# A spectral filter dealt between the matmuls of a gated MLP: its column step dealt first with pauses, down products in runs of 3, 3 and 2, and evictions and copies issued in another order

## The chip, the cores and the metric

The kernel runs on one core of a Trainium2 chip. The time is the device time of one execution in microseconds. Before the change it was 1312.53 us (median of 3 runs, 1312.05 to 1313.11). TensorE (PE) multiplies matrices, VectorE (DVE) and ScalarE (ACT) do elementwise work, GpSimd (POOL) and SyncE (SP) here only issue transfers (POOL also a few fills).

## The reference

```python
x = A_x                                   # 1 x 2048 x 576
g = _sigmoid((x * gate_w).sum(-1, keepdims=True))
a = irfft2(rfft2(x) * (w_r + 1j * w_i))   # over 2048 x 576
b = einsum(gelu(x @ w_gate) * (x @ w_up), w_down)   # hidden width 4608
return g * a + (1 - g) * b
```

Two results are mixed by a gate for each token: `a` filters the tokens in the two-dimensional Fourier domain, `b` is a gated MLP with a tanh GELU.

## The kernel before, in words

**The matmuls.** Each fp32 operand is split into a high and a low part (12 bits each), and a product is made of three matmuls, high by high, low by high and high by low. The MLP goes over two halves of the tokens (`p`), and for each over 18 blocks of 256 hidden features (`i`). The first two blocks of the first half are done plainly (`normal`, L1597). The other 34 are done in `products` (L1408): the gate and up projections of a block by seven products of sums and differences of quarters (`a11 a12 s2 s3 s1 a22 s4`, a scheme of Strassen's kind, n = 0 to 6) in place of eight. One product is two halves (s = 0, 1), each of seven matmuls with 512 columns (`seven`, L1392). Products n = 0, 2 and 3 are copied out of PSUM by ScalarE (L1478): n = 0 into another PSUM tile, from which later products go on, n = 2 and 3 into SBUF (`u`, `u3`, tiles `xraw`). Product 1 accumulates into the PSUM tile of product 0 after that was copied, and product 3 into that of product 2. `finish` (L1422) queues gelu, multiplication and the split of the hidden tile.

**Downs.** The hidden tiles of a block wait in `pend` and are multiplied by `w_down` during the next block: eight downs (`down`, L995), each for 128 tokens and of 12 matmuls with 288 columns into a PSUM tile `pdn`, of which there are two. ScalarE evicts it, scaled by 1 - g, into one of four staging tiles `stg` (L1011), and a transfer issued on POOL adds that to the result in DRAM (`put`, L982). The tuple `downs` (L1448) says how many downs follow each product: 1,1,1,1,1,1,2 in most blocks, 0,0,0,0,0,1,1 in the first of the 34 (`opening`) and 2,2,2,2,2,0,0 in the last (`end`).

**The order of work.** The order of every engine's instructions is written out by this program. After each half product and each down, `gap` (L782) is called; it counts gaps and deals out other work (`dealt`, L788): first all that `at(n, fn)` (L774) put off to this gap, then work from a generator, paid from a credit. `tick` adds 1.08 times the estimated TensorE time to the credit, VectorE work takes its estimated cost off, and the credit is capped (2.0, in the column stage 2.4). A generator yields a cost, or None when it wants to go on only at a later gap. The generator (`branch`, L1585) does the whole spectral part: row transforms on VectorE, columns, inverse rows, and last the adds of `a` to the result (`adds`, L703). What is left of it is dealt without limit in the last block, at n = 5 (L1493).

**The column stage** (`columns`, L290). The transform over tokens is finished in 16 steps `kb`. A step makes a first complex product on TensorE (`product`, L347: six matmuls with 290 columns, also into a `pdn` tile), copies it out, combines it on VectorE (L431 to L433), turns it by 90 degrees on ScalarE (`turned`, L248), multiplies by the filter (L443, L444), adds (L450 to L452), and splits the result for a second product, which is made in the next step (L438) and copied out at L441. L446 to L457 prepare the operand of the next step. Beside it a second generator (`beside`, L381, in `side`) does the radix-4 column butterflies (`column_four`, L253) and twiddles (`column_twiddles`, L269) of the tiles to come and of those done; a step waits at L447 until its tiles are made. While this stage runs (`ops["ahead"]`), `dealt` takes from the side work first, and from the step only if credit is left (L798 to L817). Evictions of downs are then not issued in `down` but kept in `post`, which is emptied at the end of the gap or just before the turn (L435). Otherwise `down` issues the eviction itself, ahead of its gap.

Of the kernel before, what the change touches and what calls it, by code (L numbers as in the profile page):

```python
# [27 lines left out]
ROWS = 5120  # L28
UNIT = ROWS // 4
RATE = 1.08  # L30
STEP = 8
FIRST = 2
APART = (13, 14, 16, 17)
PAIRS = ((2, 3, 4, 5), (6, 7, 8, 9), (10, 11, 12, 13), (14, 15, 16, 17), (0, 1))
# [126 lines left out]
def _build(nc, tc, a):  # L161
    with ExitStack() as ctx:
# [72 lines left out]
        def copy(o, i):  # L235
            act.activation(o, i, AF.Copy)  # L236
# [53 lines left out]
        def columns():  # L290
# [52 lines left out]
            def step(us=0.0):  # L343
                credit[0] -= us
                yield None
# [75 lines left out]
            for kb in range(16):  # L421
                was, more = kb > 0, kb + 1 < 16
                v = product(0, kb, xh, xl)
                if was:
                    copy(yh, vs)
                yield from step()
                copy(zr, v[:, 1, :NK])
                copy(t0, v[:, 0, :NK])
                yield from step()
                if was:  # L430
                    vec.tensor_tensor(yl, vs, f(yh), ALU.subtract)  # L431
                vec.tensor_tensor(zi, t0, zr, ALU.subtract)
                vec.tensor_tensor(zr, t0, zr, ALU.add)  # L433
                yield from step(1.67 if was else 0.91)
                while post:  # L435
                    post.pop(0)()
                turned(vs, z, 1.0)
                u = product(1, kb - 1, yh, yl) if was else None  # L438
                yield from step()
                if was:  # L440
                    copy(two(tile_of(kb - 1)), u[:, :, :NK])  # L441
                    done[0] = kb - 1
                vec.tensor_tensor(z, z, w0, ALU.mult)  # L443
                vec.tensor_tensor(vs, vs, w1, ALU.mult)  # L444
                yield from step(1.52)
                if more:  # L446
                    while made[0] < (kb + 1) // 4:  # L447
                        yield None
                    copy(xh, tile_of(kb + 1))
                vec.tensor_tensor(z, z, vs, ALU.add)  # L450
                vec.tensor_tensor(vs2[:, 0], zr, zi, ALU.add)
                vec.tensor_tensor(vs2[:, 1], zr, zi, ALU.subtract)  # L452
                at(1, lambda kb=kb: load_ww(kb + 1, 0))
                at(2, lambda kb=kb: load_ww(kb + 1, 1))
                yield from step(1.67)
                if more:
                    vec.tensor_tensor(xl, tile_of(kb + 1), f(xh), ALU.subtract)  # L457
                yield from step(0.76)
                yield from waits(STEP - 7)
            copy(yh, vs)  # L460
            yield None
            vec.tensor_tensor(yl, vs, f(yh), ALU.subtract)
# [325 lines left out]
        def dealt():  # L788

            count[0] += 1  # L790
            while later and later[0][0] <= count[0]:
                later.pop(0)[1]()
            if aux:
                aux.pop(0)()
            credit[0] = min(credit[0], cap[0])
            if not gens:
                return
            ahead = side and ops.get("ahead")  # L798
            while ahead and credit[0] > 0:
                v = next(side[0], None)  # L800
                if v is None:
                    break
                credit[0] -= v
            while credit[0] > 0:
                try:
                    v = next(gens[0])
                except StopIteration:
                    gens.pop(0)
                    v = None
                if v is None:  # L810
                    while side and not ahead and credit[0] > 0:
                        v = next(side[0], None)
                        if v is None:
                            break
                        credit[0] -= v
                    return
                credit[0] -= v  # L817
# [177 lines left out]
        def down(prev, t):  # L995

            p, i, tb = prev[:3]
            u = 8 * p + 4 * tb + t
            v = ps_dn()
            for part in range(2):  # L1000
                down_mm((v[:, 0, 0:HD], v[:, 1, 0:HD]), prev, t, part)
            if t == 3:
                for _, hold, _ in prev[3]:
                    h = hold[0]
                    if any(h is x for x in base + extra):
                        free_h.append(h)
            if p == 0 and i == 0 and tb == 0:
                copy(held(u).rearrange("p (c k) -> p c k", c=2), v[:, :, 0:HD])
            else:
                assert ops.get('released', 0) > min(dnn[0], 3)  # L1010
                out = lambda: put(u, lambda o: act.activation(o.rearrange("p (c k) -> p c k", c=2), v[:, :, 0:HD], AF.Copy,  # L1011
                                                              scale=omg[:, u:u + 1]), i == 0, i)
                if ops.get("ahead"):
                    post.append(out)
                else:
                    out()
            behind[0] = t % 2 == 0
            gap()
            behind[0] = False
# [388 lines left out]
        def products(b, k):  # L1408
# [4 lines left out]
            made = {}  # L1413
            opening, end, turn = k == 0, k == len(b.groups) - 1, (p, i) == (0, NBLK - 1)
            if opening:
                at(6, lambda: credit.__setitem__(0, credit[0] - 2.0))
                for q in range(2 * len(PAIRS) - 2):
                    t = (free_low[:, 0:7 * P] if q % 2 == 0 else wtb[:, 0:7 * P]).rearrange("p (m k) -> p m k", m=7)
                    for n, fn in zip((-4, 6, 8, 9, 10), tail_piece(q + 2, t)):
                        at(max(1, n + 12 * q), fn)  # L1420
# [25 lines left out]

            fore, acc = ([f() for f in fs] for fs in ((ps_gu, ps_gu), (lambda: ps_x(0), lambda: ps_x(1)))[::1 - 2 * (k % 2)])
            downs = (0, 0, 0, 0, 0, 1, 1) if opening else (2, 2, 2, 2, 2, 0, 0) if end else (1, 1, 1, 1, 1, 1, 2)  # L1448
            for n, (name, nd) in enumerate(zip(("a11", "a12", "s2", "s3", "s1", "a22", "s4"), downs)):
                m = n + 3  # L1450
                b.prep(k + m // 7, m % 7)
# [20 lines left out]
                    fore = [ps_x(s) for s in range(2)] if k % 2 else [ps_gu() for _ in range(2)]  # L1472
                ps = acc if n in (2, 3, 5) else fore
                for s in range(2):
                    soon = opening and n in (0, 2)
                    b.seven(ps[s], k, n, name, s, n in (0, 4), (lambda n=n, s=s: copy((acc, None, u)[n][s], ps[s])) if soon else None)
                    if n in (0, 2, 3) and not soon:
                        copy((acc, None, u, u3)[n][s], ps[s])  # L1478
                    elif n in (4, 6):
                        at(0 if end else 1, lambda x=(u3, u)[n // 2 - 2][s], y=ps[s]: add(x, y))  # L1480
# [6 lines left out]
                    at(2, lambda name=name: swap(name))  # L1487
                if n in (1, 4, 5, 6):
                    finish(*{1: ("c11", fore, gl[0]), 4: ("c22", u3, u3[0]), 5: ("c21", acc, gl[1]), 6: ("c12", u, u[0])}[n])
                for _ in range(nd):  # L1490
                    if pend:
                        down(*pend.pop(0))
# [214 lines left out]
```

## Time and profile before

The profiled execution took 1312.65 us, its span (first to last instruction) 1310.9 us. Busy time by stretch, in us:

| stretch | what runs beside the MLP | PE | DVE | ACT | granted PE clock | share of DMA time |
|---|---|---|---|---|---|---|
| 100 to 558 | row transforms, operands of the second half | 458.00 | 418.03 | 287.79 | 1.00 | 0.90 |
| 558 to 912 | column stage and what follows it | 349.60 | 285.21 | 264.36 | 1.00 | 0.98 |
| 912 to 1250 | inverse rows | 338.00 | 315.50 | 195.72 | 1.00 | 0.86 |
| 1250 to 1311 | last adds, last block, end | 56.47 | 29.93 | 23.08 | 0.98 | 0.90 |

How to read the lines that follow. A line of a view of groups has the source line, the engine, the operation, what it writes and reads, shapes and count, then busy time and the mean of one in ns, then the idle time before it with what ended that. A line of the waits has who waited for whom, the total in us, how often, and the longest. A line of a timeline has the start, the time until the end of the last of the merged instructions, the instruction and the count, and idle time in brackets. A line of the chain of waits has start and length. The ends of matmuls are modelled, so the pace of TensorE is read from starts. L236 is the helper `copy` on ScalarE, so copies are told apart by their tiles.

### The profile page before, as it was taken

How to read it: one execution, taken by the hardware profiler on the slowest of the kernel's cores; microseconds unless marked ns; L12 is line 12 of the kernel's file. 1: busy time of each engine (PE TensorE's matmuls, PEld its weight loads, DVE VectorE, ACT ScalarE, POOL GpSimd, SP SyncE). 2: the span in 40 equal slices, each digit the busy share in tenths (PEclk: the TensorE clock that was granted, in tenths of full speed). 3: DMA queues.
4: the chain of work that ended last, by engine and by line, in shares of the span. 5: the costliest groups of instructions: out<-in, count | busy, mean ns of one | idle time of the engine just before them, and what ended most of it. 6: DMA issues, size and time to landing. Idle time of an engine off the chain costs nothing.

```text
span 1310.9 us, 20543 instructions
## 1 busy us (share of the span) xinstructions
PE 1299.9 (99%) x7210; PEld 1150.1 (88%) x7210; DVE 1134.5 (87%) x1734; ACT 831.6 (63%) x1405; POOL 307.7 (23%) x392
## 2 busy tenths in 40 slices
PE   9999999999999999999999999999999999999998
PEld 7888888888888888888888888888888888888888
DVE  7899999988999998778888878778999977999954
ACT  5665655657565667678687878766555566565552
POOL 0011212122221211124321333333331231212151
PEclk9999999999999999999999999999999999999999
DMA  9779999897777799969988999999997798877797
GB/s 350 240 204 235 263 257 244 190 286 138 138 145 146 143 320 367 296 174 272 398 250 202 217 258 222 252 224 209 176 184 152 140 217 206 182 158 141 150 188 194
DMA packets 202537, 285.94 MB, mean 218 GB/s; under 512 B 18177, under 2 KB 118657, under 8 KB 201665
## 3 DMA queue, kind: packets, MB, share of 16 engines
q0 software_dynamic: 64848, 110.13, 49.4%
q1 hardware_dynamic: 137152, 174.06, 40.9%
q8 instruction: 56, 0.92, 0.3%
q10 hardware_dynamic: 432, 0.44, 0.1%
q14 instruction: 49, 0.39, 0.1%
HBM read 157.87 MB, written 137.88 MB: 226 GB/s over the span
## 4 chain that ended last, share of the span: by engine, by line
PE 86%; DMA 5%; DVE 4%; ACT 3%; issue 1%; SPq 1%; DVEq 0%; ACTq 0%
PE pdn L978 31%; PE px L1399 22%; PE pgu L1399 22%; PE px L1401 4%; PE pgu L1401 4%; DMA gub<-tails 1%; PE pdn L351 1%; DMA ye<-stg 1%; DMA gub<-ws 1%; DMA home<-rows 1%; ACT gub L236 0%; DMA tmp<-rows 0%; ACT stg L1011 0%; DMA low<-wgu 0%; DVE gub L1383 0%
## 5 line engine op out<-in xcount | busy, mean ns | idle before, releaser
L1011 ACT ACTIVATE stg<-pdn,omg 128x576 f32<-128x576 f32 x276 | 204.6, 741 | 328.8 <-PE pdn L978 182.5
L993 POOL DMA_DIRECT2D yd<-stg x232 | 202.1, 871 | 778.4 <-ACT stg L1011 752.6
L978 PE MATMUL pdn<-dn,hb 128*128 128x288 f32 x1356 | 199.9, 294 | 1.6 <-ACT rows L236 1.4
L978 PEld LDWEIGHTS pdn<-dn,hb 128*128 128x128 f32 x1356 | 191.7, 188 | 10.7 <-ACT rows L236 2.1
L1399 PE MATMUL pgu<-xhi,gub 128*128 128x512 f32 x480 | 149.0, 392 | 0.0
L1399 PE MATMUL pgu<-til,gub 128*128 128x512 f32 x516 | 132.1, 391 | 1.0 <-ACT xraw L236 1.0
L978 PEld LDWEIGHTS pdn<-dn,ext 128*128 128x128 f32 x816 | 122.2, 188 | 9.3
L978 PE MATMUL pdn<-dn,ext 128*128 128x288 f32 x816 | 129.3, 294 | 0.0
L978 PE MATMUL pdn<-dn,gub 128*128 128x288 f32 x816 | 129.3, 294 | 0.0
L1383 DVE TENSOR_TENSOR gub<-low,gub 128x512 fp32r<-128x512 f32 x151 | 103.4, 685 | 17.5 <-ACT gub L236 15.6
L978 PEld LDWEIGHTS pdn<-dn,gub 128*128 128x128 f32 x816 | 115.4, 188 | 0.0
L1399 PEld LDWEIGHTS pgu<-til,gub 128*128 128x128 f32 x516 | 94.4, 188 | 19.1 <-ACT xraw L236 1.2
L236 ACT ACTIVATE gub<-low 128x512 fp32r<-128x512 f32 (+1 forms) x163 | 100.7, 619 | 12.3 <-DMA low<-wgu 6.1
L1399 PE MATMUL px<-xhi,gub 128*128 128x512 f32 x344 | 106.9, 392 | 1.2 <-DVE gl L1427 0.7
L1399 PE MATMUL px<-til,gub 128*128 128x512 f32 x396 | 101.2, 391 | 0.0
L1399 PEld LDWEIGHTS pgu<-xhi,gub 128*128 128x128 f32 x480 | 86.6, 188 | 14.6
L1399 PE MATMUL pgu<-xlo,gub 128*128 128x512 f32 x240 | 93.6, 390 | 0.0
L1399 PEld LDWEIGHTS px<-til,gub 128*128 128x128 f32 x396 | 72.5, 188 | 13.7
L1399 PEld LDWEIGHTS px<-xhi,gub 128*128 128x128 f32 x344 | 62.0, 188 | 12.3 <-DVE gl L1427 1.2
L978 PE MATMUL pdn<-dn,hx 128*128 128x288 f32 x444 | 70.3, 294 | 0.0
L1401 PE MATMUL pgu<-til,gub 128*128 128x512 f32 x172 | 67.1, 390 | 0.4 <-DMA gub<-tails 0.4
L1399 PE MATMUL px<-xlo,gub 128*128 128x512 f32 x172 | 67.1, 390 | 0.0
(311 smaller groups left out, 2758.6 us busy)
## 6 DMA issues: line engine op xcount, KB each, us to landing
yd<-stg POOLq DMA_DIRECT2D x232, 288.0 KB, 5.4
low<-ws SPq DMA_DIRECT2D x114, 256.0 KB, 5.4
gub<-tails SPq DMA_DIRECT2D x179, 128.0 KB, 4.9
gub<-wd SPq DMA_DIRECT2D x68, 288.0 KB, 5.4
tails<-wtb SPq DMA_DIRECT2D x28, 448.0 KB, 5.6
ye<-stg POOLq DMA_DIRECT2D x32, 288.0 KB, 5.5
yd<-ye POOLq DMA_DIRECT2D x32, 288.0 KB, 7.4
slot<-tails SPq DMA_DIRECT2D x59, 128.0 KB, 4.6
```

The costliest lines, as they stand in the source:

```text
L236: act.activation(o, i, AF.Copy)
L351: pe.matmul(v[:, al, :NK], cc[d][2 * al + q], two(x)[:, al], start=n == 0, stop=n == 2)
L978: pe.matmul(ps[half], h[:, l, c], d[:, q, half * HD:(half + 1) * HD], start=part == 0 and n == 0, stop=part == 1 and n == 2)
L993: pl.dma_start(yd[u], o, accum_op=ALU.add)
L1011: out = lambda: put(u, lambda o: act.activation(o.rearrange("p (c k) -> p c k", c=2), v[:, :, 0:HD], AF.Copy, scale=omg[:, u:u + 1]), i == ...
L1383: vec.tensor_tensor(v[:, 0:5:4], x, f(v[:, 1:4:2]), ALU.subtract)
L1399: pe.matmul(ps, l, x[:, t], start=first and t == 0 and q == 0, stop=False, skip_group_check=True)
L1401: pe.matmul(ps, w[:, 512 + P * s:512 + P * (s + 1)], xt, start=False, stop=True, skip_group_check=True)
```

## The change

In the column stage the step gets three pauses: `yield None` ahead of the emptying of `post` and the turn, `yield None` between the copy out of the second product and the multiplications, and, as before, one at the step's end. `dealt` takes one piece of the step first, in every gap and whatever the credit, and then side work for the credit that is left. Outside that stage the eviction of a down is put off by `at(1, out)`: it is still issued in the gap behind its down, but behind what was already put off to that gap. In all blocks the copies of products 0, 2 and 3 are issued inside `seven`, ahead of their gap (before, only those of 0 and 2 in the opening block were; the others came behind the gap). The downs come behind products 1, 4 and 6, in runs of 3, 3 and 2, except in the opening and the last block and while the column stage runs. In the opening block 1.5 us more are taken off the credit at gap 10.

```diff
-STEP = 8
...
                 yield from step(1.67 if was else 0.91)
+                yield None
                 while post:
                     post.pop(0)()
                 turned(vs, z, 1.0)
...
                 if was:
                     copy(two(tile_of(kb - 1)), u[:, :, :NK])
                     done[0] = kb - 1
+                yield None
                 vec.tensor_tensor(z, z, w0, ALU.mult)
                 vec.tensor_tensor(vs, vs, w1, ALU.mult)
...
                 yield from step(0.76)
-                yield from waits(STEP - 7)
+                yield None
...
             if not gens:
                 return
-            ahead = side and ops.get("ahead")
-            while ahead and credit[0] > 0:
-                v = next(side[0], None)
-                if v is None:
-                    break
-                credit[0] -= v
+            if side and ops.get("ahead"):
+                credit[0] -= next(gens[0]) or 0.0
+                while side and credit[0] > 0:
+                    v = next(side[0], None)
+                    if v is None:
+                        break
+                    credit[0] -= v
+                return
             while credit[0] > 0:
...
                 if v is None:
-                    while side and not ahead and credit[0] > 0:
+                    while side and credit[0] > 0:
...
                 if ops.get("ahead"):
                     post.append(out)
                 else:
-                    out()
+                    at(1, out)
...
             if opening:
-                at(6, lambda: credit.__setitem__(0, credit[0] - 2.0))
+                for n, us in ((6, 2.0), (10, 1.5)):
+                    at(n, lambda us=us: credit.__setitem__(0, credit[0] - us))
...
             downs = (0, 0, 0, 0, 0, 1, 1) if opening else (2, 2, 2, 2, 2, 0, 0) if end else (1, 1, 1, 1, 1, 1, 2)
+            popped = 0
...
-                    soon = opening and n in (0, 2)
-                    b.seven(ps[s], k, n, name, s, n in (0, 4), (lambda n=n, s=s: copy((acc, None, u)[n][s], ps[s])) if soon else None)
+                    soon = n in (0, 2, 3)
+                    b.seven(ps[s], k, n, name, s, n in (0, 4), (lambda n=n, s=s: copy((acc, None, u, u3)[n][s], ps[s])) if soon else None)
...
+                if not (opening or end):
+                    nd = (n + 1 + n // 6 if ops.get("ahead") else (0, 3, 3, 3, 6, 6, 8)[n]) - popped
+                    popped += max(0, nd)
                 for _ in range(nd):
                     if pend:
                         down(*pend.pop(0))
```

## The prediction

> **What bounds the kernel now.** I read the page's head first, then the waits of TensorE, then the chain of waits.
>
> ```profile
> span 1310.9 us, 20543 instructions
> PE 1299.9 (99%) x7210; PEld 1150.1 (88%) x7210; DVE 1134.5 (87%) x1734; ACT 831.6 (63%) x1405; POOL 307.7 (23%) x392
> ```
>
> TensorE is busy 99% of the span, so nothing on another engine counts unless it makes TensorE wait. The next view lists such waits behind the start.
>
> ```profile
> PE pdn L978 <- ACT rows L236: 1.4, 3, 0.5
> PE pgu L1399 <- ACT xraw L236: 1.0, 1, 1.0
> PE px L1399 <- DVE gl L1427: 0.7, 1, 0.7
> PE px L1399 <- DVE slot L1383: 0.5, 1, 0.5
> PE px L1399 <- ACT pgu L236: 0.5, 1, 0.5
> PE pgu L1401 <- DMA gub<-tails: 0.4, 1, 0.4
> PE pdn L351 <- DVE tmp L457: 0.2, 1, 0.2
> ```
>
> L1383 is in the opening block. The other six lines (eight waits, 4.2 us shown) all lie in or just behind the column stage. The chain of waits, whose long pieces are pairs of downs, says what that stage loses in all.
>
> ```profile
> 133.41 3.16 PE pdn L978 x24
> ...
> 168.43 3.16 PE pdn L978 x24
> ...
> 553.57 3.16 PE pdn L978 x24
> ...
> 937.21 3.16 PE pdn L978 x24
> ```
>
> ```profile
> 586.12 0.97 PE L351 MATMUL pdn<-tmp,xtl 128*128 128x290 f32 x6
> 586.93 0.56 PE L978 MATMUL pdn<-dn,ext 128*128 128x288 f32 x3
> ```
>
> A block without disturbance takes 35.02 us (133.41 to 168.43). From 553.57 to 937.21 there are ten blocks in 383.64 us: ten times 35.02 is 350.2, and 32 column products at 0.81 (586.12 to 586.93) are 25.9. So 7.5 us are lost there. That, and what an undisturbed block can save, is all this change can win.
>
> **Runs of downs.** Nothing is removed: 8 downs and 98 product matmuls a block stay. What changes is how often TensorE goes from one kind to the other. First a pair and a single down with the product behind each, then products with no down between.
>
> ```profile
> 133.25 3.32 PE L978 MATMUL pdn<-dn,hb 128*128 128x288 f32 x24
> 136.41 0.63 PE L1399 MATMUL pgu<-xhi,gub 128*128 128x512 f32 x2
> ...
> 139.63 1.74 PE L978 MATMUL pdn<-dn,hb 128*128 128x288 f32 x12
> 141.20 0.63 PE L1399 MATMUL pgu<-xhi,slot 128*128 128x512 f32 x2
> ...
> 144.40 0.30 PE L978 MATMUL pdn<-dn,hb 128*128 128x288 f32 x1
> ```
>
> ```profile
> 87.13 1.52 PE L1399 MATMUL px<-til,slot 128*128 128x512 f32 x6
> ...
> 91.89 0.62 PE L1399 MATMUL px<-xhi,gub 128*128 128x512 f32 x2
> ```
>
> By the starts, three half products without a down take 4.76, or 3.17 for a whole one. Behind a single down it is 3.20 (141.20 to 144.40), behind a pair 3.22 (136.41 to 139.63), and the pair takes 3.16 where two singles take 3.14. So a single run costs 0.03 and a pair 0.07. A block loses 6 x 0.03 + 0.07 = 0.25 now. A run of three is not in the trace: if its product pays as behind a pair, it costs 0.05 and some 0.03 for its two joints; if the cost grows on, 0.08 + 0.04; if joining is free, 0.05. Two of these and a pair make 0.23, 0.31 or 0.17. Over 24 blocks (34, less opening, end and eight in the column stage) that is a gain of 1.9 to a loss of 1.4. I take 0.23, nearest to the row of the pair: a gain of 0.02 x 24 = 0.5 us.
>
> [...]
>
> **What hides the closed gaps.** With three downs in a row, the third needs the first one's PSUM tile (two exist), so ScalarE's eviction must be done within one down. The trace of before has no third down, but a pair followed by a product gives the time it would have.
>
> ```profile
> 239.87 0.96 PE L978 MATMUL pdn<-dn,hb 128*128 128x288 f32 x6
> ...
> 241.46 0.63 PE L1399 MATMUL px<-xhi,slot 128*128 128x512 f32 x2
> ```
>
> ```profile
> 240.12 0.74 ACT L1011 ACTIVATE stg<-pdn,omg 128x576 f32<-128x576 f32 x1 [3.03 <-issue]
> ```
>
> ```profile
> L1011 ACT ACTIVATE stg<-pdn,omg 128x576 f32<-128x576 f32 x105 | 78.0, 743 | 144.9 <-PE pdn L978 82.3 <-issue 56.4 <-ACT gub L236 2.6
> ```
>
> The first down ends at 239.87, its eviction runs from 240.12 to 240.86, and a third down would start at 241.46: 0.60 to spare, 0.54 after the 0.06 that a release takes (below). The group is that of 100 to 558 us: 144.9 us idle before 105 evictions, nearly all of it for TensorE, so ScalarE usually stands ready. Copying "a gap on" puts this gap's own ScalarE work (a gelu, a high part) ahead of the eviction; it can run while the down is still on, so it costs nothing unless ScalarE is behind. Then what is queued behind the eviction is late too, and TensorE waits.
>
> The products now also follow each other with no down between: the second accumulates into the PSUM tile that ScalarE copies after the first, one half product (1.59) later. A heavy place shows it, TensorE (the half behind the copied one) first, then ScalarE.
>
> ```profile
> 252.63 1.52 PE L1399 MATMUL pgu<-til,gub 128*128 128x512 f32 x6
> ```
>
> ```profile
> 252.38 1.41 ACT L236 ACTIVATE tmp<-rows 128x289 f32<-128x289 f32 x2
> 253.68 0.60 ACT L236 ACTIVATE xraw<-pgu 128x512 f32<-128x512 f32 x1
> ```
>
> The copy ends at 254.28, and with no down the half that needs it would start 1.59 after 252.63, at 254.22: late. Issued ahead of those two row copies it could start at 252.88 (0.25 behind the half's end, as the eviction) and end at 253.48, 0.7 to spare. So the reordered copies hide what the runs expose. Of 48 third downs I count two as late, 0.35 each (priced below): a loss of 0.7; the ends are 0 and 48 x 0.35 = 16.8. POOL issues each staging transfer behind its eviction; the four staging tiles come round after eight gaps (12.7 us) at the least, so three evictions in a row need no further wait there.
>
> **The column stage.** Three of its waits are for the copy of the second column product out of PSUM. Two ScalarE timelines and the matmul that waited:
>
> ```profile
> 746.52 0.69 ACT L250 ACTIVATE wtb<-wtb 64x580 f32<-64x580 f32 x1 [2.17 <-DVE wtb L433]
> ...
> 748.48 0.64 ACT L236 ACTIVATE rows<-pdn 128x580 f32<-128x580 f32 x1
> ```
>
> ```profile
> 669.37 0.69 ACT L250 ACTIVATE low<-rows 64x580 f32<-64x580 f32 x1
> ...
> 670.79 0.65 ACT L236 ACTIVATE rows<-pdn 128x580 f32<-128x580 f32 x1
> ```
>
> ```profile
> 670.15 0.95 PE L978 MATMUL pdn<-dn,hx 128*128 128x288 f32 x6
> 671.50 0.40 PE L978 MATMUL pdn<-dn,hb 128*128 128x288 f32 x1 [0.40 <-ACT rows L236]
> ```
>
> At 670 the turns of the side work (L250, `low`) were issued ahead of the copy; dealing the column step first puts the copy ahead. At 746 the turn of the step itself stood idle 2.17 us for VectorE; the first pause gives VectorE a gap more before it. The copy ended at 671.44 and the matmul began at 671.50 (release 0.06); it was due 6 x 0.13 after 670.15, at 670.94, so 0.40 shown cost 0.56. I price a wait at its length plus 0.16, and a very short one, with the matmul behind it that is slow too, at 0.35.
>
> The three copies cost 1.4 + 0.5 = 1.9 and go. The product copy (L1399 for `xraw`) costs 1.15 and goes by being ahead, and so does `pgu`, 0.65. L457 costs 0.35 and goes with the side work behind it. The transfer (0.6) and L1427 (0.9) have causes that stay: a DMA, and VectorE behind after the stage. These are 5.6 of the 7.5; of the other 1.9 (slow first matmuls, waits that the modelled ends hide) I let half go, 0.9. Gained: 4.9. The step now takes ten gaps instead of eight, so pairs of downs meet its products in new places: I charge two waits of 0.35, 0.7. Net 4.2; ends: 7.5 gained, or 1.5 lost if new places cost as the old and two more like `xraw` come.
>
> The pauses make the stage longer in gaps: 16 steps x (10 x 35.02/22 + 2 x 0.81) = 281 us, against 230 with eight, while it takes 297 now (16 first products below, 15 steps from 558.2 to 836.4, 18.5 each), since it also stands still for the side work. With the side work now second I expect minus 10 to plus 15. The tail has room for that:
>
> ```profile
> L351 PE MATMUL pdn<-tmp,xtl x96: 291/297/405, 558.2 to 836.4; 128*128 128x290 f32 x96
> ```
>
> ```profile
> L718 POOL DMA_DIRECT2D yd<-tmp x3: 1082/1191/1527, 1264.7 to 1270.5; - x3
> ```
>
> ```profile
> low<-yd SPq DMA_DIRECT2D x4, 288.0 KB, 5.7
> ...
> yd<-tmp POOLq DMA_DIRECT2D x3, 288.0 KB, 8.2
> ```
>
> ```profile
> L1048 DVE SCALAR_TENSOR_TENSOR low<-pdn,omg,low x4: 817/818/819, 1295.4 to 1300.1; 128x576 f32<-128x576 f32 x4
> ```
>
> The last spectral add is issued at 1270.5 and what it adds to is read back for 1295.4, 24.9 us later; its transfer (8.2) and the reading back (5.7) lie between, so 11 us of delay cost nothing. The opening's larger debt of credit moves VectorE work behind the place of the L1383 wait: 0.
>
> **The sum.** Against the profiled execution's 1312.65 (1.75 around its span): -0.5 + 0.7 - 4.2 = -4.0, 1308.65. The median of the runs is 0.12 lower, so 1308.5.
>
> **Rivals.** *The waits only move* (27%): every wait has another cause next in line, VectorE's lag or the step's new phase, and the stage still loses 6 to 8. For it: DMA and L1427 stay. Against: most causes are an order on ScalarE that the change turns round. Then 1311 to 1313, no change. That the change does not do what it says ends here too: if the step waits for side work anyway, dealing it first alters little.
>
> *The third down waits* (12%), the other side: evictions held by one more ScalarE operation. From 0.54 late on it decides; one operation of 0.60 (the copy at 253.68) is enough, at 0.35 a place. At half of 48 places 8.4, less what the rest wins (4.7), +3.7: 1316.2. For it: the eviction moves behind the gap's work. Against: the idle time before L1011. The Trainium skill (PSUM — Partial Sum Buffer, Summary: rules for kernel authors) says "Evacuate promptly"; by that rule this rival is the likeliest, while the trace shows slack of 0.54.
>
> *The stage grows past the tail's room* (6%): by 20 us, 9 over; 1308.5 + 9 = 1317.5.
>
> **The numbers.** A measurement of this kernel tells about 0.2% (2.6 us) from no change, so faster is under 1309.9. The forecast (55%) lies there, its own range 1305 to 1309.9; with the edge of the first rival, faster 0.57; same 0.26; slower 0.17. The range leaves out the best 5% or so and most of the two slow rivals: 1305.0 to 1315.5.
>
> **What would show it.** Right: no TensorE wait on `rows` or `xraw` from 558 on; blocks outside the stage at 35.00 to 35.04; evictions still beginning 0.25 behind a down. Wrong: a new row "PE pdn L978 <- ACT stg L1011" with dozens of entries; a period over 35.1; last adds after 1282; ten blocks round the stage still near 383.6.

## The result and the profile after

The changed kernel took 1325.16 us (median of 5 runs, 1324.21 to 1327.94) where the kernel before took 1312.53 (1312.05 to 1313.11). The ratio is 1.0101, with a 95% interval of 1.0087 to 1.0114: the change costs 12.6 us. The profiled execution took 1327.20, 2.0 above the median, so what its trace adds up to is a little more than 12.6. The head of its page:

```profile
span 1325.4 us, 20539 instructions
PE 1305.0 (98%) x7210; PEld 1153.4 (87%) x7210; DVE 1134.8 (86%) x1734; ACT 835.9 (63%) x1405; POOL 309.4 (23%) x392
```

The span grew by 14.5 us (from 1310.9) at the same number of instructions on TensorE, VectorE, ScalarE and POOL; PE's busy time grew by 5.1. So nothing was added, and TensorE waits longer or runs slower. The waits of TensorE behind the start:

```profile
PE pdn L350 <- DVE tmp L458: 6.5, 3, 3.4
PE px L1402 <- ACT pgu L235: 3.3, 2, 2.4
PE pdn L981 <- ACT stg L1014: 1.9, 3, 0.9
PE pdn L350 <- DMA xtl<-col: 1.5, 1, 1.5
PE pdn L350 <- DVE tmp L430: 0.7, 1, 0.7
PE pgu L1404 <- DMA gub<-tails: 0.2, 1, 0.2
```

`rows`, `xraw`, `gl` and `slot` are gone from the list. The row that was the smallest in before (L457 there, now L458) is the largest, 6.5 us in place of 0.2: the **first** column product waits for its operand from VectorE (the 0.7 for L430 is the second product's). The copy for `pgu` comes late at two other places, 3.3 in place of 0.5. New is that a third down waits for the eviction of the first (L1014), and once the transfer of the step's matrices (`xtl<-col`, 1.5) is late. That last wait is there with the stage as before too (1.9 in e1 below) and not in e2, so it isn't the new dealing that makes it; its cause was not traced.

To see where the 14.5 us lie I added up, for each stretch, the time from start to start of consecutive matmuls over 227 ns for one with 512 columns and over 132 ns for one with 288 or 290. This "loss" holds waits, slow matmuls and joints alike.

| stretch (us) | before | after |
|---|---|---|
| 0 to 100 | 3.3 | 2.7 |
| 100 to 555, row transforms and operands | 1.2 | 5.2 |
| 555 to 910, column stage | 9.0 | 15.5 |
| 910 to 960, behind the stage | 0.2 | 4.7 |
| from 960 | 1.0 | 1.2 |

So there are three places: +4.0, +6.4 and +4.6; the rest gave back 0.5. Each of them is one of the parts of the change at work.

**The column stage.** VectorE first, then TensorE, at one of the three waits for L458:

```profile
746.80 0.76 DVE L282 SCALAR_TENSOR_TENSOR rows<-rows,low 128x580 f32<-128x580 f32 x1 [3.88 <-ACT low L250]
747.48 0.69 DVE L1386 TENSOR_TENSOR gub<-low,gub 128x512 fp32r<-128x512 f32 x1
...
752.17 0.76 DVE L458 TENSOR_TENSOR tmp<-rows,tmp 128x580 fp32r<-128x580 f32 x1
```

```profile
750.47 0.42 PE L350 MATMUL pdn<-tmp,xtl 128*128 128x290 f32 x2
752.98 0.81 PE L350 MATMUL pdn<-tmp,xtl 128*128 128x290 f32 x4 [2.08 <-DVE tmp L458]
```

L282 is a twiddle of the side work. VectorE stood still 3.88 us for the turn on ScalarE that it needs, and then worked through what was queued, without a pause from 746.80 on; L458, the low part of the step's operand, was in that queue. Ahead of the other two waits (692.5 and 790.9) side work itself fills VectorE, four additions of a butterfly (L258, 3.1 us) and eight (L258 and L265, 6.2 us). Meanwhile the step was dealt on, a piece in each gap, so its product came in TensorE's order before VectorE had made the operand. At 692.5 the same wait lasted 3.4 us, and the matmuls behind it ran at half clock:

```profile
697.20:700.50 3.30, 3.30 (x10) 2.55 (x9) 3.01 (x5) 1.85 (x4) 0.53 (x1) 0.51 0.61 167
```

This is a stretch with its length and the busy time of PE, PEld, DVE, ACT and POOL; the number behind these, 0.51, is the granted clock of TensorE, as a share of its full speed. For 3.3 us it was 0.51, which costs 3.3 x 0.49 = 1.6 us on top of the wait.

**Behind the stage.** ScalarE, then TensorE:

```profile
917.50 0.64 ACT L235 ACTIVATE slot<-low 128x512 fp32r<-128x512 f32 x1 [6.08 <-DVE low L1371]
918.04 0.72 ACT L1014 ACTIVATE stg<-pdn,omg 128x576 f32<-128x576 f32 x1
918.66 0.62 ACT L1435 ACTIVATE xraw<-xraw 128x512 f32<-128x512 f32 x1
919.18 0.73 ACT L1014 ACTIVATE stg<-pdn,omg 128x576 f32<-128x576 f32 x1
919.80 0.72 ACT L235 ACTIVATE rows<-tmp 128x289 f32<-128x289 f32 x1
920.31 0.70 ACT L235 ACTIVATE pgu<-px 128x512 f32<-128x512 f32 x1
```

```profile
918.32 0.39 PE L1404 MATMUL px<-til,gub 128*128 128x512 f32 x1
921.06 0.73 PE L1402 MATMUL px<-xhi,gub 128*128 128x512 f32 x2 [2.35 <-ACT pgu L235]
```

The high part of a weight block (`slot<-low`) needs L1371 from VectorE and stood 6.08 us for it. Both evictions, put off to behind the gap's other work, and the copy of product 0 were queued behind it, and ran one after another once it was through. TensorE stopped for 2.35 us, and its granted clock was 0.86 over the 12 us from 915 on.

**Third downs.** TensorE, then ScalarE, at the first of the two in the stretch from 100 to 555:

```profile
299.04 0.95 PE L981 MATMUL pdn<-dn,gub 128*128 128x288 f32 x6
300.88 1.06 PE L981 MATMUL pdn<-dn,ext 128*128 128x288 f32 x6 [0.90 <-ACT stg L1014]
```

```profile
297.11 1.25 ACT L740 ACTIVATE tmp<-tmp 128x576 f32<-128x576 f32 x1
...
298.85 1.27 ACT L740 ACTIVATE tmp<-tmp 128x576 f32<-128x576 f32 x1
299.99 0.21 ACT L740 ACTIVATION_READ_ACCUMULATOR tmp<-tmp 128x1 f32 x1
300.09 0.74 ACT L1014 ACTIVATE stg<-pdn,omg 128x576 f32<-128x576 f32 x1
```

The second down ended about 299.83 and the third started at 300.88. L740 sums rows for the gate: 1.27 us and 0.21 to read the sum, one in each gap for eight tiles of tokens. The eviction of the first down was queued behind one of them.

### The profile page after: what moved, and what is told of

Its sections match the earlier page's. It is cut to its first block, busy times and chain, and to the rows that moved or that the text cites. A ratio compares the mean times of both kernels' runs of the same rounds, so it can differ in the third digit from the quotient of the medians.

```text
span 1325.4 us, 20539 instructions
## 1 busy us (share of the span) xinstructions
PE 1305.0 (98%) x7210; PEld 1153.4 (87%) x7210; DVE 1134.8 (86%) x1734; ACT 835.9 (63%) x1405; POOL 309.4 (23%) x392
## 4 chain that ended last, share of the span: by engine, by line
PE 85%; DVE 6%; DMA 5%; ACT 3%; issue 1%; SPq 0%; DVEq 0%; ACTq 0%
PE pdn L981 30%; PE pgu L1402 21%; PE px L1402 21%; PE pgu L1404 4%; PE px L1404 4%; PE pdn L350 2%; DMA away<-wtb 1%; DMA xtl<-col 1%; DMA gub<-wd 1%; DMA kept_s<-wtb 1%; DMA home<-rows 1%; PE px L917 1%; PE pgu L917 0%; ACT stg L1014 0%; DMA kept_a<-tmp 0%
## 5 line engine op out<-in xcount | busy, mean ns | idle before, releaser
L1014 ACT ACTIVATE stg<-pdn,omg 128x576 f32<-128x576 f32 x276 | 204.3, 741 | 211.2 <-PE pdn L981 162.7
L981 PEld LDWEIGHTS pdn<-dn,ext 128*128 128x128 f32 x816 | 119.1, 188 | 6.6 <-ACT stg L1014 2.6
L1402 PEld LDWEIGHTS px<-til,gub 128*128 128x128 f32 x396 | 73.0, 188 | 14.5 <-ACT xraw L235 0.2
```

What stands on the lines that cost most here:

```text
L981: pe.matmul(ps[half], h[:, l, c], d[:, q, half * HD:(half + 1) * HD], start=part == 0 and n == 0, stop=part == 1 and n == 2)
L1402: pe.matmul(ps, l, x[:, t], start=first and t == 0 and q == 0, stop=False, skip_group_check=True)
```

## The experiments

All run times below are medians with the kernel before beside them on the same chip (1312.4 to 1312.9); ratios are to it and are taken over all runs, so they are not exactly the quotients of the medians. "Loss" is that of the table above, by stretch; the column "end" is from 1250 us on. Three kernels (e5 no runs, e11 copies ahead alone, e10 copies and step) don't compute the reference: they issue copies ahead with a single down behind each product outside the stage. Their traces show one place where that breaks an order: behind the opening block, VectorE makes the low part of a hidden tile (L963, `hb<-xraw`) only after the copy of product 2 has begun to overwrite the tile that it reads. In e11 the copy starts at 113.5 and the low part at 114.1; in the kernel before it was 112.9 and 112.1. Whether other sums differ too was not traced. They have the same 7210 matmuls, and only their times are used.

| kernel | median us | ratio [95%] | 100-555 | 555-910 | 910-960 | end |
|---|---|---|---|---|---|---|
| before | 1312.5 | 1 | 1.2 | 9.0 | 0.2 | 0.2 |
| after | 1325.16 | 1.0101 [1.0087, 1.0114] | 5.2 | 15.5 | 4.7 | 0.2 |
| e1 after, stage as before | 1318.01 | 1.0033 [1.0019, 1.0047] | 4.8 | 11.3 | 0.9 | 0.3 |
| e2 before, new dealing and pauses | 1317.18 | 1.0033 [1.0020, 1.0046] | 1.2 | 13.3 | 0.2 | 0.2 |
| e3 after, step on credit | 1329.60 | 1.0119 [1.0092, 1.0146] | 5.4 | 16.0 | 4.4 | 0.2 |
| e4 after, eviction at once | 1323.45 | 1.0080 [1.0063, 1.0096] | 4.6 | 16.3 | 0.5 | 0.2 |
| e5 after, no runs | 1321.14 | 1.0066 [1.0051, 1.0081] | 1.4 | 16.4 | 0.6 | 0.2 |
| e7 before, new dealing alone | 1320.95 | 1.0066 [1.0051, 1.0081] | 1.2 | 17.1 | 0.1 | 0.2 |
| e8 before, pauses alone | 1343.09 | 1.0233 [1.0216, 1.0250] | 1.2 | 13.0 | 0.3 | 28.6 |
| e9 e2, side turns used later | 1317.99 | 1.0043 [1.0028, 1.0058] | 1.2 | 10.4 | 0.1 | 4.1 |
| e13 e2, side pauses elsewhere | 1318.23 | 1.0043 [1.0029, 1.0056] | 1.2 | 5.2 | 6.7 | 2.2 |
| e12 after, side turns used later | 1320.26 | 1.0054 [1.0039, 1.0070] | 6.0 | 12.8 | 0.1 | 1.6 |
| e11 before, copies ahead alone | 1317.28 | 1.0029 [1.0017, 1.0041] | 1.2 | 12.3 | 2.5 | 0.2 |
| e10 copies and step | 1308.61 | 0.9970 [0.9959, 0.9981] | 1.2 | 4.9 | 0.1 | 0.2 |
| e14 step, third turn used later | 1311.13 | 0.9992 [0.9983, 1.0001] | 1.2 | 7.5 | 0.1 | 0.2 |
| e15 e14, copies ahead in the stage | 1308.89 | 0.9975 [0.9966, 0.9985] | 1.8 | 5.2 | 0.1 | 0.2 |
| e16 after, mended | 1319.53 | 1.0059 [1.0047, 1.0071] | 4.4 | 13.2 | 0.1 | 0.3 |

### e1: the changed kernel with the stage as before

```diff
-                yield None
                 while post:
...
-                yield None
                 vec.tensor_tensor(z, z, w0, ALU.mult)
...
-            if side and ops.get("ahead"):
-                credit[0] -= next(gens[0]) or 0.0
...
+            ahead = side and ops.get("ahead")
+            while ahead and credit[0] > 0:
...
```

> The changed kernel with the column stage as before: side work dealt first, the step only on credit, no new pauses; runs of 3, 3 and 2, evictions put off and copies ahead stay. Theory S (the loss is made in the column stage, by a step that is dealt whatever the credit): the 8 us of first products that wait for L458 go, and 1315 to 1318 is left, that is 3 to 5 over the kernel before, for third downs and the place behind the stage. Rival O (the loss is made by runs and put-off evictions): 1322 or more, with the wait of TensorE for evictions or copies at 5 us or more.

It took 1318.01: 7.2 us less than the changed kernel. The loss of the stage falls from 15.5 to 11.3, that behind the stage from 4.7 to 0.9, and that from 100 to 555 stays at 4.8. So the stage's edits cost the larger part, also by what they leave behind the stage, and the third downs have nothing to do with them.

### e2: the kernel before with the new dealing and the pauses, nothing else

The diff is that of the change for `columns` and `dealt`.

> The kernel before with the column stage of the changed one alone (step first in every gap, three pauses). Theory S: 1318 to 1322, with waits of the first column product for L458 of some 6 us or more. Rival O: within 2 us of the kernel before, since the stage then saves about what it costs.

1317.18, ratio 1.0033. The prediction has a net gain of 4.2 for the stage, 1.8 of it (1.15 and 0.65) by the copies ahead, which are not in e2; so it has a gain of 2.4 for this part, and it is a loss of 4.3 in the stage (13.3 for 9.0). Its waits, the first three rows:

```profile
PE pdn L351 <- DVE tmp L459: 2.9, 3, 1.4
PE px L1403 <- ACT xraw L236: 2.5, 2, 1.8
PE px L1403 <- ACT pgu L236: 1.2, 1, 1.2
```

The waits on `rows` are gone here too. The operand of the first product comes late, as in the changed kernel, and the copies of products, not yet ahead of their gap, come late as well.

### e3: the step dealt first, but only on credit

```diff
-                credit[0] -= next(gens[0]) or 0.0
+                if credit[0] > 0:
+                    credit[0] -= next(gens[0]) or 0.0
```

> The changed kernel, but the step is dealt first only while credit is left (as everything else is). Theory S: it was the missing credit that let VectorE's queue fall behind TensorE, so the waits for L458 (6.5 us shown) fall under 1.5 us and the time falls by 6 to 9, to 1316 to 1319. Rival P (the places of the pauses, or the order of step and side work, are the cause whatever the credit): less than 3 us change.

1329.60, not faster than the changed kernel, and the waits on L458 are 8.2 us in place of 6.5. That the step is dealt without credit is not the cause; this idea falls.

### e4: evictions issued at once outside the stage

```diff
-                    at(1, out)
+                    out()
```

> The changed kernel with evictions of downs issued at once, ahead of their gap, as before. If the put-off eviction causes the long third-down waits (1.16 and 1.05 us) and the wait behind the stage (2.35 us shown, and the half clock after it): 3 to 6 us faster than the changed kernel, 1319 to 1322. Rival: the runs alone cause them, and less than 1.5 us changes.

1323.45. The loss behind the stage falls from 4.7 to 0.5: the place at 917 goes when the evictions are not put off. The stage (16.3) and the stretch from 100 to 555 (4.6) stay. A third down still waits, as ScalarE shows, since L740 lies ahead of the eviction in its queue either way:

```profile
299.45 1.25 ACT L740 ACTIVATE tmp<-tmp 128x576 f32<-128x576 f32 x1
300.61 0.19 ACT L740 ACTIVATION_READ_ACCUMULATOR tmp<-tmp 128x1 f32 x1
300.70 1.35 ACT L1014 ACTIVATE stg<-pdn,omg 128x576 f32<-128x576 f32 x2
```

### e5: the changed kernel without runs

```diff
-                    nd = (n + 1 + n // 6 if ops.get("ahead") else (0, 3, 3, 3, 6, 6, 8)[n]) - popped
+                    nd = (n + 1 + n // 6) - popped
```

> The changed kernel with one down behind each product as before, everywhere; evictions put off, copies ahead and the new column stage stay. Theory R (the loss outside the column stage, 3.5 us from 100 to 555 us in three of the kernels so far, and 4.6 just behind the stage, comes from closing the gaps, where a ScalarE that is late for any reason stops TensorE): the loss from 100 to 555 falls from 5.2 to about 1.2 us, and the time to 1317 to 1320, near that of the stage alone (1317.2). Rival (the put-off evictions or the copies cause it): no more than 2 us below the changed kernel.

1321.14. The loss from 100 to 555 falls from 5.2 to 1.4, so the 3.8 us there come from the runs. The stage loses 16.4, no less than before this edit. The loss behind the stage is gone here as well (0.6): by e4, e5 and e1 that place needs the eviction put off, the run, and the new order of the stage ahead of it. These three are not enough: e12 below has them all and loses 0.1 there. What else it takes was not traced.

### e7 and e8: the two halves of the stage's change, each alone

e7 is the kernel before with the new dealing and without the two pauses; e8 has the pauses, and side work first as before.

> The kernel before, with only the dealing changed: one piece of the column step first in every gap, then side work; no new pauses (eight gaps a step). Theory T (VectorE stands still for side turns on ScalarE while the step goes on by the clock): without pauses the step is even further ahead of VectorE, so first and second products wait more than with them: 1318 to 1324. Rival P (the pauses do the harm): back to 1312 to 1314.

> The kernel before with only the two further pauses in the step, side work first as before. Theory T: nothing that TensorE waits for comes earlier than before, so 1310 to 1313.5, with fewer waits for the copy out of the second product. Rival P: 1316 or more.

e7 loses 17.1 in the stage, more than with the pauses (13.3): the pauses do help the step when it is dealt first. e8 takes 1343.09. Its stage loses 13.0 (7.4 of it at one late copy of a product), but it ends late. First products, the last adds, and the wait at the end:

```profile
L351 PE MATMUL pdn<-tmp,xtl x96: 292/298/303, 558.2 to 907.4; 128*128 128x290 f32 x96
...
L720 POOL DMA_DIRECT2D yd<-tmp x3: 2643/2879/3215, 1311.5 to 1312.6; - x3
```

```profile
PE pdn L980 <- DVE low L1050: 25.8, 1, 25.8
```

The last first product comes 71 us later than before (907.4, 836.4) and the last add 42 us later (1312.6, 1270.5); TensorE waits 25.8 us in the last block. This is the third rival of the prediction, the stage that outgrows the tail's room. It is real, but not in the changed kernel, where dealing the step first holds the stage's length.

### e9 and e13: less side work between operand and product, in two ways

Both are e2 with more pauses in the side work. e9 puts them between a turn and its use, e13 in the same number ahead of the sums and turns.

```diff
             turned(y, x1, float(sgn))
             yield None
+            yield None
...
+            yield None
             for o in range(1, 4):
+                if o == 3:
+                    yield None
+                    yield None
```

```diff
             sp, y = tmps
+            yield None
...
+            for _ in range(3):
+                yield None
             for o in (1, 2):
                 turned(tmps[o % 2], T[at[o]], math.sin(angle(o)))
```

> The stage alone (step first, three pauses, on the kernel before), and in the side work one to two further pauses between a turn on ScalarE and the VectorE operation that needs it. Theory T: VectorE no longer stands still for side turns (17.7 us in the changed kernel's stage, to under 5), the waits of the first product for its operand (2.9 us shown) fall under 1, and the time to 1312 to 1314.5. Rival (the amount of VectorE work between operand and product, not its standing still): 1316 or more.

> The stage alone with just as many further pauses in the side work as in the run that put its turns later, but ahead of the side work's turns and sums, not between a turn and its use. Theory T (VectorE's standing still for a turn is what makes the first product wait): those waits stay, 2 to 4 us shown, and VectorE still stands 10 us or more for the side turns. Rival (the side work is merely thinned out by the pauses): waits under 0.5 us as with the turns later. The time says little, since both lengthen the stage: 1317 to 1321.

Neither is faster than e2. In both the waits of the first product fall from 2.9 to 0.2, whichever place the pauses have. In e13 VectorE still stands 8.5 us for the side work's turns, in the waits of VectorE from 558 to 910:

```profile
DVE rows L286 <- ACT low L251: 8.5, 7, 2.4
```

In e2 this row was 13.3, so e13 shortens the standing too and doesn't separate the two theories as it was meant to. With the turns of the butterflies (L266 in e2) the standing is 15.0 us in e2, 11.4 in e13 and 12.7 in e7, and e7 has the longest waits for operands (3.2 and 1.8); so the standing alone doesn't order them. The timelines of e2 show both causes. At its first wait VectorE had stood 2.20 us for a side turn just ahead of the operand, L459:

```profile
610.20 0.76 DVE L283 SCALAR_TENSOR_TENSOR rows<-rows,low 128x580 f32<-128x580 f32 x1 [2.20 <-ACT low L251]
...
612.08 0.76 DVE L459 TENSOR_TENSOR tmp<-rows,tmp 128x580 fp32r<-128x580 f32 x1
```

At its second, at 720.3, VectorE had worked without a pause since 712.36, four additions of a butterfly (L259, 3.2 us) among it. Either way side work lies in VectorE's queue ahead of the operand, and pauses of either kind shift and spread it. But the side work then ends later. The steps wait for it, no column product is made for some 30 us (in e9 from 764.1 to 793.8), and what is saved is paid for at a late copy of a product (`xraw`) and at the end. In e9 that copy lies in the stage (3.7 us at 767, with the half clock behind it most of its 10.4), in e13 behind it (6.7 with the half clock that follows), and the end costs 4.1 and 2.2. The rows of e13:

```profile
PE pgu L1406 <- ACT xraw L236: 3.5, 1, 3.5
PE pdn L985 <- DVE low L1055: 1.8, 1, 1.8
```

### e12: the changed kernel with the side turns used later

The first edit of e9 on the changed kernel.

> The changed kernel, whole, with the side turns later (one to two pauses between a turn and its use). Theory T: the waits for L458 (6.5 us shown, and a stretch at half clock behind one of them, 1.8) fall under 1, and what TensorE loses from 555 to 910 from 15.5 to about 9; the waits outside the stage stay (9 us from 100 to 555 and 910 to 940), and the last adds come later. 1317 to 1321. Rival: 1323 or more with the waits in place.

1320.26, 4.9 us less than the changed kernel. The waits on L458 are gone from its list, and those behind the stage too; the loss of the stage is 12.8, since a first product now waits once for an eviction (`stg`, 3.1 us shown, at 798.7), which was queued behind the high part of a weight block that stood 3.31 us for VectorE.

### e11 and e10: the copies ahead

e11 is the kernel before with the copies of products 0, 2 and 3 ahead of their gap; e10 has the new dealing and the pauses as well, and of e9's pauses only the two ahead of the use of the third turn.

```diff
-                    soon = opening and n in (0, 2)
+                    soon = n in (0, 2, 3)
```

> The kernel before with only the copies of products 0, 2 and 3 issued ahead of their gap in all blocks. If it takes away the waits for `xraw` (1.0 shown) and `pgu` (0.5 shown), as the prediction had it: 1310 to 1311.5. Rival (what is behind the copy in ScalarE's queue is late instead): 1312 to 1314.

> A version meant to be good: one down behind each product and evictions at once, as before; step first with three pauses, copies ahead, and two pauses between the third side turn and its use. If the waits for the first product and for copies go and the last adds come by 1284: 1307 to 1311. If the stage gets too long for the tail, or the side turns still hold VectorE: 1314 to 1318.

e11 alone is slower than either of its theories had it (1317.28, with runs from 1313.69 to 1318.85; its stage loses 12.3, to a late transfer of 2.4 with a stretch at half clock behind it, and to the old waits on `rows`). e10 takes 1308.61 and loses 4.9 in the stage. Taken together the parts do what the prediction hoped for the stage, once the side work is spread by two pauses and no more.

### e14 and e15: which part brings it, and a version that beats both kernels

e14 is e10 without the copies ahead. e15 has them in the column stage alone.

```diff
+                if o == 3:
+                    yield None
+                    yield None
                 x, t, c = T[at[o]], tmps[o % 2], math.cos(angle(o))
...
-                    soon = opening and n in (0, 2)
+                    soon = opening and n in (0, 2) or ops.get("ahead") and n in (0, 2, 3)
```

> The kernel before with the step dealt first, the three pauses, and two more pauses ahead of the use of the side work's third turn; copies, evictions and runs as before. Theory (the first product waits because more VectorE side work is dealt between the operand and the product than fits, pauses in the side work thin it out): the waits on the operand fall from 2.9 us shown to under 1, the stage loses 5 to 9 us in place of 13.3, the time is 1310 to 1314. Rival (the gain of the version with copies ahead came from the copies, not from thinning): the stage still loses 11 or more, 1316 to 1318.

> As the run before it, and the copies of products 0, 2 and 3 ahead of their gap in the column stage alone. Theory (both parts are needed in the stage: product copies that wait behind the step's own work stop TensorE, and side work between operand and product does): the stage loses about 5, the time is 1308 to 1311, faster than the kernel before by 0.2 to 0.3 per cent. Rival (copies ahead matter outside the stage only): as the run before it, within 1 us.

The two pauses alone bring the stage from 13.3 to 7.5 and the time from 1317.18 to 1311.13, no different from the kernel before (0.9992 [0.9983, 1.0001]). At the place of e2's first wait the side work's third use of a turn now lies behind the operand, which is ready 1.1 us before TensorE gets to the product:

```profile
608.44 0.76 DVE L462 TENSOR_TENSOR tmp<-rows,tmp 128x580 fp32r<-128x580 f32 x1
...
609.71 0.76 DVE L286 SCALAR_TENSOR_TENSOR rows<-rows,low 128x580 f32<-128x580 f32 x1
```

The wait behind the butterfly stays (1.0 shown, at 719.6). Of the 5.8 us that the stage gains over e2, the waits for the operand are 2.2 and those for product copies 2.9. The copies ahead in the stage bring it on to 5.2 and 1308.89, a ratio of 0.9975 [0.9966, 0.9985]: faster than before by 3.5 us. Both times came out as the first of the two theories had them. In the waits of e15 the copies have left the list, but for 0.3 us:

```profile
PE pdn L354 <- DVE tmp L462: 1.1, 1, 1.1
PE pgu L1406 <- ACT px L236: 0.3, 1, 0.3
```

### e16: the changed kernel with stage and eviction mended, the runs kept

The two pauses of e14 and the edit of e4 on the changed kernel.

> The changed kernel with the two more pauses in the side work, and evictions issued at once outside the stage. Theory (the three losses are separate and add up): the stage falls from 15.5 to 5 to 9, the wait behind it from 4.7 to 0.5, the third downs between 100 and 555 us stay at 4 to 5: 1312 to 1316, slower than the run with copies in the stage by the 4 or so of the runs of three. Rival (the losses are not separate, since the runs of three set where the stage's gaps fall): over 1319.

1319.53, where 1312 to 1316 was expected of separate losses. Two of the three terms came as expected: 0.1 behind the stage, 4.4 from 100 to 555. The stage did not. It loses 13.2, of which 6.0 at one place, ScalarE first:

```profile
771.18 0.68 ACT L249 ACTIVATE low<-rows 64x580 f32<-64x580 f32 x1 [8.63 <-DMA rows<-away]
771.89 0.68 ACT L250 ACTIVATE low<-rows 64x580 f32<-64x580 f32 x1
772.60 0.74 ACT L1017 ACTIVATE stg<-pdn,omg 128x576 f32<-128x576 f32 x1
```

```profile
773.39 1.09 PE L353 MATMUL pdn<-tmp 128*128 128x290 f32 x3 [5.81 <-ACT stg L1017]
```

A turn of the side work was issued before its tile had come back from DRAM. The eviction was queued behind it, and the step's second product (`pdn<-tmp` without `xtl`) needed that PSUM tile. From 774 to 777 the granted clock was 0.50, from 777 to 780 0.63: 3 x 0.50 + 3 x 0.37 = 2.6 more. Without this place some 4.6 is left of the stage's loss. So the wait on the first product's operand is mended here too (0.2 left), but another of the same family came in its place; which of the edits moved the transfer or the turn into each other's way, I have not shown.

## Why the prediction was wrong

**Right.** The regrouping: an undisturbed block takes 35.00 where it took 35.02, by the chain of waits, and 0.02 was predicted.

```profile
132.80 3.16 PE pdn L981 x24
167.80 3.16 PE pdn L981 x24
```

The old waits of the stage went, as predicted; those on `rows` go with the dealing alone (e2), and stay without it (e11). The stage did not get longer: 567.9 to 845.8 is 277.9 us, 558.2 to 836.4 was 278.2. The tail had the room that was worked out: the last adds come at 1291.0 where they came at 1270.5, 20.5 later in a span 14.5 longer, and TensorE doesn't wait for them. So the sign "last adds after 1282" was there, but they cost nothing.

```profile
L350 PE MATMUL pdn<-tmp,xtl x96: 291/297/406, 567.9 to 845.8; 128*128 128x290 f32 x96
...
L719 POOL DMA_DIRECT2D yd<-tmp x3: 1196/1217/2092, 1284.5 to 1291.0; - x3
```

The price of a wait, its shown length plus 0.16, held as well: the wait of 2.08 at 752.98 cost 2.25.

**The step that failed most, in the column stage: "L457 costs 0.35 and goes with the side work behind it", and with it "I charge two waits of 0.35, 0.7".** The wait for L457 (now L458) was to go; it grew from 0.2 shown to 6.5, and the charge of 0.7 stood in the sum for all that dealing the step first could cost. For the stage -4.2 was predicted and +6.4 measured; without the copies ahead, in e2, -2.4 and +4.3. The working counted only waits that were there and asked which would go. It did not ask what they had held back. In the kernel before, side work first held up the step, so that its product, too, came later in the written order: its steps are 13.6 to 27.5 us apart, from first product to first product, and those of e2 16.8 to 20.0. Dealing the step first makes the product come by the gaps; the VectorE work in front of its operand is still ahead of it, and not behind it as that step of the prediction had it. The old waits were for copies on ScalarE, and what came back, larger, is the wait for the operand from VectorE. By the timelines of the changed kernel, e2 and e14 it is side work in VectorE's queue ahead of the operand, in part standing for its turn, in part at work; how much is due to each is not shown. The first rival ("The waits only move", with "VectorE's lag") named the mechanism, but gave it the old size. Of the stage's 6.4, 1.7 are the late transfer, which no run explains.

**The third downs: "two as late, 0.35 each".** The count was right for 100 to 555 (at 299.7 and 511.3), a third is at 888.9. The size was not: by the measure of the table 1.06, 0.95 and 0.34, and a late copy of product 0 at 526.6 for 1.15. The slack of 0.54 was measured at a place where ScalarE stood ready, and the mean idle time before L1011 hid the places with L740 (1.27 and 0.21). Here the wait for ScalarE's whole next operation is the price, not a short wait's 0.35. By e5 the runs cost 3.8 us from 100 to 555, about half of what the second rival has, though at three places and not at half of 48. On this the Trainium skill (PSUM — Partial Sum Buffer, Summary: rules for kernel authors), with its "Evacuate promptly", was on the right side: a few places without slack lose some eight times the 0.5 that the runs save (24 blocks at 0.02). Issuing the evictions promptly, e4, is not enough where L740 is in the queue already.

**"It costs nothing unless ScalarE is behind."** It was behind once, for 6.08 us at 917.5, and TensorE lost 4.6 us there, with the half clock behind it. e4 and e5 each take it away.

**Missing altogether: the half clock.** Behind the long waits at 692 and 918, and at 767 in e16, TensorE ran on at a lower clock, which cost 1.6 to 2.6 us each. No term of the sum had that.

The three losses came together, and the range, which let one rival come true at a time, ended at 1315.5.

## What to carry to other kernels

Ask of a wait that you take away what it held back: if two engines that work in their written order feed a third, an earlier consumer needs an earlier producer, and the producer's queue has to be read at that place, not its mean idle time. Slack that is measured at one place (0.54 us here) has to be compared with the longest single operation that can be queued in front of the eviction (1.27 + 0.21). Pauses and priorities in a hand-dealt order are worth trying one at a time and in small numbers: dealing the step first, with its pauses, two pauses in the side work and the copies ahead in the stage, won 3.5 us, while more pauses, or runs, gave it back.

## What was not expected of the hardware

A single wait of TensorE was enough to halve its clock for a while, and the length of the wait alone doesn't say whether it does. In the changed kernel the granted clock fell behind shown waits of 2.35 and 3.4 us and stayed at 1.00 behind one of 2.08. In e7 it is the other way round: it stayed at 1.00 behind a wait of 2.4 us that ended at 625.2, and fell to 0.50 behind one of 1.9 us that ended at 766.2.

```profile
625.20:628.20 3.00, 3.00 (x17) 2.70 (x18) 3.00 (x5) 2.11 (x5) 1.18 (x3) 1.00 1.02 409
767.00:770.40 3.40, 3.40 (x9) 2.63 (x8) 3.33 (x7) 2.94 (x6) 1.92 (x2) 0.50 1.09 198
```

In e3 the clock stayed at 1.00 even behind a wait of 3.0 us that ended at 793.9. What else decides was not shown. Behind the wait of 3.5 us in e13 it was low for longer:

```profile
920.00:924.00 4.00, 4.00 (x10) 2.89 (x10) 4.00 (x7) 3.46 (x7) 0.85 (x1) 0.50 0.96 172
```

TensorE was granted 0.50 of its clock while it was busy all the time, from 920 to 924. The Trainium skill (TensorE: Matmul & The Clock Gate, What's actually happening) says that the clock falls to half after at least one idle window of about 3.4 us, and rises again after a busy one. The length of the slow stretch agrees (3.4 us at 0.50 in e7); the idle time that suffices was less here, 1.9 us shown and 2.16 from start to start (764.05 to 766.21, in e7). In this kernel a wait with the half clock behind it cost 1.6 to 2.6 us more than its length.
